# Turning the first batch's token blocks by 16-bit halves and a transposing DMA, in an attention and mixer kernel on one core

## The chip, the cores and the metric

One NeuronCore of one Trainium2 chip. The metric is the device time of one execution in microseconds; 492.01 is the median of three runs before the change (491.93 to 492.79).

## The reference, cut to what matters

```python
x = attn(q, k, v)                       # banded attention, 2 batches, 768 tokens, 512 wide
xt = x.transpose(0, 2, 1)
h = np.maximum(xt @ w_tok1, 0.0) @ w_tok2          # 768 -> 256 -> 768
u = x + h.transpose(0, 2, 1)
h2 = np.maximum(u @ w_ch1, 0.0) @ w_ch2            # 512 -> 1536 -> 512
x = u + h2
...                                     # a third part: rotation by x @ w_theta, a second token mix, w_ch
```

Everything is fp32. The kernel writes each fp32 operand as a high and a low part and makes a product of three matmuls (high x high, high x low, low x high).

## The kernel before, in words

The program has a band branch and a dense branch (`tc.If(band)`, L933); with these inputs the band branch runs. Every engine has its own list of instructions, in the order in which the code is written (`manual_schedule`), and crosses the branch's end by itself.

Inside the branch `attention_band` (L412) walks 24 units of two token blocks each. In unit u PE makes the scores of u, the transposes `t` of u-1 (L485) and the value products `o` of u-2 (L407). Table `fill` puts pieces of the first token mix behind units: `token_part` (L752) adds one block's three matmuls to `mm1`, whose two tiles (`tb` 0 and 1) are emptied by ACT and DVE into `h1`; `token_row` (L772) makes the six matmuls `mm_b_s` of one block of the second product, and DVE adds them to `x` (L787). For batch 0 both lie within the branch. Its turned blocks follow there too: `turn_row` (L789) makes four PE transposes `ut` (L792) of block s, ACT casts them to the high part (L739) and DVE subtracts for the low part (L743). For batch 1 the first product ends the branch and the second, `token_mix2` (L1020), begins the code behind it, with one `tick` after every second block.

Behind it `channel_mix` (L1030) runs 24 steps: `up` makes `gp` from the turned columns (a half of 512 tokens, blocks 0 to 3, then one of 256, blocks 4 and 5), ACT (L707) and DVE (L709) empty it into `g`, and `down` adds 18 matmuls to `h`. `gp` has two PSUM banks, in turn. Batch 1's blocks are turned there by another path: POOL copies a block's 16-bit halves apart (`halves_out`, L799), SP issues a transposing DMA (L803), POOL copies the halves together again (`halves_join`, L809), then the same ACT cast and DVE subtraction, one block in a step.

The weights arrive as 64-bit words. A `tick` moves every job under way by one phase and starts one: ACT scales (L140, L141), DVE joins (L146, L149) and POOL adds (L150), ACT makes the high part (L158), DVE the low part (L161). `need` ticks until a step's weights are there. `Banks` hands the `acc` tiles out over three PSUM tags in turn.

Of the kernel before, what the change touches and what calls it, by code (L numbers as in the profile page):

```python
# [15 lines left out]
F32 = mybir.dt.float32  # L16
# [4 lines left out]
ALU = mybir.AluOpType  # L21
# [26 lines left out]
GRAIN = 64  # L48
SHIFT = 48
# [34 lines left out]
class Build:  # L84
# [327 lines left out]
    def attention_band(self, pairs_pool, first, h1):  # L412
        nc, tc = self.nc, self.tc
# [5 lines left out]
        with tc.tile_pool(name="au", bufs=2) as up, tc.tile_pool(name="aa", bufs=2) as ap:  # L419
# [118 lines left out]
            N = len(units)  # L538
            fill = collections.defaultdict(list)

            def mix1(b, tb, s, tag):
                return functools.partial(self.token_part, tag, h1, b, tb, s)

            def mix2(s):
                return functools.partial(self.token_row, "m", h1, 0, s)

            def columns(s):
                return functools.partial(self.turn_row, "t", 0, s)

            for n in range(2 * NS):  # L550
                tb, s = divmod(n, NS)
                fill[half + 2 + n // 2].append(mix1(0, tb, s, "m"))
            for s in range(NS):
                fill[N - 4 + s].append(mix2(s))
            for s in range(4):
                fill[N - 2 + s].append(columns(s))
            for tb in range(NT):
                for s in range(NS - 2):
                    fill[N + 1].append(mix1(1, tb, s, "s"))
            self.token_jobs()  # L560
            pairs[order[1]] = self.load_qk(pairs_pool, *order[1], bufs=2)
            for u in range(N + 2):
# [36 lines left out]
                    if oi + 2 < len(order):  # L599
                        pairs[order[oi + 2]] = self.load_qk(pairs_pool, *order[oi + 2], bufs=2)  # L600
            for tb in range(NT):
                for s in range(NS - 2, NS):
                    mix1(1, tb, s, "s")()
            for s in range(4, NS):
                columns(s)()

    def attention_dense(self, pairs_pool, first, h1):

# [3 lines left out]
        with tc.tile_pool(name="du", bufs=2) as up, tc.tile_pool(name="dm", bufs=1) as mp:  # L612
# [3 lines left out]
            t = first  # L616
            for b in range(B):
                for hp in range(NHP):
# [5 lines left out]
                    for i in range(NS):  # L624
# [67 lines left out]
                                    po[:, 0], at, t["v"][:, k], j, k == 0, k == NS - 1  # L692
                                )
                        self.finish_rows(up, po, 1, b, hp, i, "d" + n)
            for bb in range(B):
                for tb in range(NT):
                    for s in range(NS):
                        self.token_part("m", h1, bb, tb, s)
            for s in range(NS):
                self.token_row("m", h1, 0, s)  # L700
                self.turn_row("t", 0, s)

# [66 lines left out]
        if s == NS - 1:  # L769
            self.evac_split(h1[b][:, 0, tb], h1[b][:, 1, tb], mm1, relu=True)  # L770

    def token_row(self, tag, h1, b, s):  # L772

        ps = self.ps.tile([P, E], F32, name="mm2_%d_%d" % (b, s), tag=tag)
        cs = slice(s * P, (s + 1) * P)
        self.mm3(
            ps,
            [
                (
                    (r(self.w2h[:, t, cs]), r(self.w2l[:, t, cs])),  # L780
                    (h1[b][:, 0, t], h1[b][:, 1, t]),
                )
                for t in range(NT)
            ],
        )
        x = self.x[b][:, s, :]
        self.nc.vector.tensor_tensor(out=x, in0=ps, in1=x, op=ALU.add)  # L787

    def turn_row(self, tag, b, s):  # L789
        pt = self.ps.tile([P, NE, P], F32, name="ut_%d_%d" % (b, s), tag=tag)  # L790
        for d in range(NE):
            self.nc.tensor.transpose(pt[:, d, :], self.x[b][:, s, d * P : (d + 1) * P], self.ident)  # L792
        self.columns_split(b, s, pt)

    def halves_out(self, src, t, copy):

# [34 lines left out]
    def split_tile(self, n, name, narrow):  # L831

        if n % 3 != 1:
            return self.ws.tile([P, 2, E], F32, name=name, tag="w", bufs=9)
        m = n // 3
        size = 2 * E + (GRAIN if m == 4 else (SHIFT, GRAIN - SHIFT)[m % 2])
        c0 = (0 if m % 2 else SHIFT) if narrow else (GRAIN - SHIFT if m % 2 else 0)
        w = self.ws.tile([P, size], F32, name=name, tag="n%d" % m)
        return w[:, c0 : c0 + 2 * E].rearrange("p (l e) -> p l e", l=2)

    def early_tile(self, name, i, shift):
        if i != 2:
# [39 lines left out]
    def run(self):  # L882
        nc, tc, dram = self.nc, self.tc, self.dram
        with ExitStack() as es:
# [8 lines left out]
            for b in range(B):  # L893
# [4 lines left out]
            self.mm1 = {}  # L898
# [109 lines left out]
    def moe(self, es, a8s, w12p, h1):  # L1008
        tc = self.tc
        ws = es.enter_context(tc.tile_pool(name="ws", bufs=1, side="right"))  # L1010
        self.moe_jobs(ws, w12p)
        self.prefetch()
        self.token_mix2(h1)
        a8s.close()
        gp = es.enter_context(tc.tile_pool(name="g", bufs=2, side="right"))
        xtp = es.enter_context(tc.tile_pool(name="xt", bufs=1, side="right"))
        tp = es.enter_context(tc.tile_pool(name="tb", bufs=1, side="right"))
        self.channel_mix(gp, PhaseB(self, xtp, tp, gp))

    def token_mix2(self, h1):  # L1020
        for s in range(NS):
            self.token_row("acc", h1, 1, s)
            if s % 2:
                self.tick()

    def columns_out(self, pb, s):
        t = self.turning[s] = pb.scratch("ut_%d" % s, ("cut", "xt0", "xt1")[s % 3])
        self.halves_out(self.x[1][:, s, :], t, self.nc.gpsimd.tensor_copy)

    def channel_mix(self, gp, pb):  # L1030
        nc = self.nc
# [19 lines left out]
        def down(b, k, g):  # L1051
            self.need(self.wc_job[k, 1])
            c2 = self.wc[k][1]
            if k == 0:
                ho[b] = [
                    self.ps.tile([P, E], F32, name="h2_%d_%d" % (b, s), tag="acc") for s in range(NS)
                ]
            for s in range(NS):
                cs = slice(s * P, (s + 1) * P)
                self.mm3(  # L1060
                    ho[b][s],
                    [((g[:, 0, cs], g[:, 1, cs]), (r(c2[0]), r(c2[1])))],
                    first=k == 0,
                    last=k == NF - 1,
                )
# [5 lines left out]
        self.turning = {}  # L1071
# [4 lines left out]
        for i, (b, k) in enumerate(steps):  # L1076
            nxt = up(*steps[i + 1]) if i + 1 < len(steps) else None
            if b == 0:
                if 0 <= k - 4 < NS:
                    self.columns_split(1, k - 4, self.turning.pop(k - 4)[:, 1])  # L1080
                if 0 <= k - 3 < NS:
                    self.halves_join(self.turning[k - 3], nc.gpsimd.tensor_copy)
                if 0 <= k - 2 < NS:
                    self.columns_out(pb, k - 2)
            if b == 1:
                for act, n in plan.get(k, ()):
                    act(n)
            down(b, k, g)
            if b == 1 and k < NF - 1 and k not in (5, 6, 7):
                self.tick()  # L1090
            if (b, k) == (0, NF - 2) or b == 1:
                self.gate += 1
            g = nxt
# [285 lines left out]
```

## Time and profile before

| | us |
|---|---|
| median of three runs | 492.01 (491.93 to 492.79) |
| profiled execution | 491.69 |
| its span, first to last instruction | 489.9 |
| PE busy | 482.7 (99%) |
| DVE busy | 320.0 (65%) |
| ACT busy | 262.6 (54%) |
| POOL busy | 179.2 (37%) |

Busy shares are means over stages. On PE, which overlaps its matmuls, a busy share says little about how well it is fed; the waits, the chain that ended last and the timeline of the stretch say more. Times in the rows are microseconds from the span's start; the chain of waits gives PE's steps by their ends, so it stands some 0.2 us behind the timeline.

### The profile page before, as it was taken

To read this page: it belongs to the slowest core of one execution; us is meant where nothing else is said; L and a number is where in the kernel's file an instruction comes from. 1 tells how busy PE (TensorE), PEld (TensorE's weight loads), DVE (VectorE), ACT (ScalarE), POOL (GpSimd) and SP (SyncE) were. 2 spreads that over 40 slices of the span, in tenths; PEclk is the share of its full clock that TensorE was granted. 3 is DMA by queue.
4 is the path that set the end of the run, shared out by engine and by line. 5 is a ranking of instruction groups with operands and counts; after the bars stand their busy time and mean duration, and the time that the engine had idled before them with its cause. 6 is when DMAs were issued, how large, how long until landed. Compare 5 with 4: busy or idle time off the path is not lost.

```text
span 489.9 us, 7655 instructions
## 1 busy us (share of the span) xinstructions
PE 482.7 (99%) x2836; PEld 409.9 (84%) x2836; DVE 320.0 (65%) x679; ACT 262.6 (54%) x482; POOL 179.2 (37%) x187
## 2 busy tenths in 40 slices
PE   8999999999999999999999999999999999999997
PEld 4888888788888888888888888888888889988896
DVE  4688788854776699606756564687998876351442
ACT  6798777723565554204569464646776556322010
POOL 7346433430443565401423241334554643333000
PEclk9999999999999999999999999999999999999999
DMA  6686864301453545302444322433310111000012
GB/s 193 208 266 218 281 207 119 127 2 39 147 169 107 165 133 155 83 1 86 145 134 149 88 51 64 136 95 93 79 23 21 40 26 23 21 23 22 23 72 100
DMA packets 49022, 50.66 MB, mean 103 GB/s; under 512 B 20944, under 2 KB 39888, under 8 KB 48976
## 3 DMA queue, kind: packets, MB, share of 16 engines
q1 hardware_dynamic: 48976, 50.08, 34.4%
q8 instruction: 25, 0.41, 0.4%
q14 instruction: 21, 0.17, 0.1%
HBM read 42.21 MB, written 3.15 MB: 93 GB/s over the span
## 4 chain that ended last, share of the span: by engine, by line
PE 86%; DVE 5%; ACT 5%; POOL 1%; DMA 1%; issue 1%; SPq 0%; DVEq 0%; ACTq 0%
PE gp L97 20%; PE h L97 18%; PE y L97 13%; PE v L97 7%; PE mm L97 7%; PE o L407 6%; PE t L485 5%; PE s L438 5%; PE th L97 5%; DMA q<-q 1%; ACT cut_xt L809 1%; DVE x L1068 1%; DVE w L1159 1%; POOL s L1185 1%; ACT cvt L140 1%
## 5 line engine op out<-in xcount | busy, mean ns | idle before, releaser
L150 POOL TENSOR_TENSOR cvt<-cvt,cvs 128x512 int32<-128x512 int32 (+1 forms) x57 | 75.0, 1317 | 176.9 <-DVE cvt L149 146.9
L97 PE MATMUL h<-wc,g 128*128 128x512 f32 x432 | 102.0, 390 | 0.0
L97 PE MATMUL gp<-xh,wc 128*128 128x512 f32 (+1 forms) x384 | 96.1, 333 | 0.0
L97 PEld LDWEIGHTS h<-wc,g 128*128 128x128 f32 x432 | 79.5, 188 | 15.6
L97 PEld LDWEIGHTS gp<-xh,wc 128*128 128x128 f32 x384 | 66.7, 188 | 8.6 <-DVE g L709 0.2
L709 DVE SCALAR_TENSOR_TENSOR g<-gp,g 128x512 fp32r<-128x512 f32 (+1 forms) x48 | 26.7, 555 | 61.4 <-ACT g L707 61.4
L97 PE MATMUL gp<-xl,wc 128*128 128x512 f32 (+1 forms) x192 | 63.1, 334 | 0.0
L97 PE MATMUL y<-wri,s 128*128 128x512 f32 (+1 forms) x288 | 51.6, 334 | 0.4 <-POOL s L1185 0.4
L707 ACT ACTIVATE g<-gp 128x512 fp32r<-128x512 f32 (+1 forms) x48 | 23.4, 488 | 52.9 <-PE gp L97 52.9
L97 PE MATMUL y<-wri,z 128*128 128x512 f32 (+1 forms) x288 | 51.5, 333 | 0.0
L485 PE MATMUL t<-ident,e 128*128 128x128 f32 x176 | 48.1, 285 | 1.0 <-ACT at L497 1.0
L97 PEld LDWEIGHTS y<-wri,s 128*128 128x128 f32 x288 | 43.5, 188 | 6.4 <-POOL s L1185 0.8
L97 PEld LDWEIGHTS y<-wri,z 128*128 128x128 f32 x288 | 43.7, 188 | 5.8
L146 DVE SCALAR_TENSOR_TENSOR cvs<-cvt,cvs 128x512 int32<-128x512 int32 (+1 forms) x57 | 43.2, 758 | 0.0
L97 PEld LDWEIGHTS gp<-xl,wc 128*128 128x128 f32 x192 | 36.0, 188 | 4.8
L485 PEld LDWEIGHTS t<-ident,e 128*128 128x128 f32 x176 | 31.7, 184 | 8.9 <-ACT at L497 2.7
L451 DVE CUSTOM_DVE_ANT_0 e<-s,base 128x256 f32<-128x256 f32 (+1 forms) x96 | 32.9, 398 | 8.5 <-PE s L438 7.0
L140 ACT ACTIVATE cvt<-raw 128x512 f32<-128x512 f32 (+1 forms) x57 | 37.1, 652 | 2.3 <-issue 2.3
L141 ACT ACTIVATE cvs<-raw 128x512 int32<-128x512 uint16 (+1 forms) x57 | 37.3, 654 | 0.0
L97 PE MATMUL th<-s,xt 128*128 128x512 f32 x144 | 34.9, 391 | 0.1
L1162 ACT ACTIVATE w<-w 128x512 f32<-128x512 f32 x12 | 7.6, 633 | 48.3 <-DVE w L1159 48.3
L407 PE MATMUL o<-v,at 128*128 128x65 f32 x192 | 32.3, 252 | 0.0
(111 smaller groups left out, 843.1 us busy)
## 6 DMA issues: line engine op xcount, KB each, us to landing
raw<-w_ch SPq DMA_DIRECT2D x28, 512.0 KB, 4.1
raw<-w_tok SPq DMA_DIRECT2D x21, 512.0 KB, 4.2
k<-k SPq DMA_DIRECT2D x7, 480.0 KB, 5.6
v<-v SPq DMA_DIRECT2D x8, 384.0 KB, 3.9
out<-o SPq DMA_DIRECT2D x11, 256.0 KB, 2.0
q<-q SPq DMA_DIRECT2D x7, 384.0 KB, 4.9
raw<-w_theta SPq DMA_DIRECT2D x4, 512.0 KB, 4.0
a<-v SPq DMA_DIRECT2D x8, 240.0 KB, 4.7
```

What stands on the lines that cost most here:

```text
L97: self.nc.tensor.matmul(out, lhsT=a, rhs=b, start=first and i == 0, stop=last and i == n - 1)
L140: nc.scalar.activation(out=f(t), in_=f(top), func=AF.Copy, scale=2.0**-111)
L141: nc.scalar.activation(out=s, in_=nxt, func=AF.Copy, scale=2.0**-13)
L146: nc.vector.scalar_tensor_tensor(out=s, in0=t, scalar=-(1 << 31), in1=s, op0=ALU.bitwise_and, op1=ALU.bitwise_or)
L150: nc.gpsimd.tensor_tensor(out=t, in0=t, in1=s, op=ALU.add)
L407: self.nc.tensor.matmul(po[:, j * OW : j * OW + D + 1], lhsT=at, rhs=v[:, j * (D + 1) : (j + 1) * (D + 1)], start=first, stop=last,)
L438: nc.tensor.matmul(ps[j][:, ii, c0:], lhsT=t["q"][pj, i * P : (i + 1) * P], rhs=kf[pj, i * KW - P + c0 : i * KW + P], start=True, stop=True,)
L451: nc.vector.tensor_tensor_reduce(out=e, in0=ps[j][:, ii, c0:], in1=self.base[2 * hp + j][min(i, 1)], op0=ALU.add, op1=ALU.min, scale=-SCAL ...
L485: nc.tensor.transpose(pt[:, ii, c, :], e[j][:, ii, c * P : (c + 1) * P], self.ident)
L707: nc.scalar.activation(out=hi, in_=ps, func=AF.Relu if relu else AF.Copy)
L709: nc.vector.scalar_tensor_tensor(out=lo, in0=ps, scalar=0.0, in1=f(hi), op0=ALU.max, op1=ALU.subtract)
L1162: nc.scalar.activation(out=a, in_=t, func=AF.Abs)
```

## The change

Batch 0's six blocks no longer go over PE. `token_mix2`, behind the branch, opens with POOL's halves of blocks 0 to 3, then their joins, then the same for blocks 4 and 5; the DMA is issued by `halves_out`. Batch 1's second product is taken in two passes over the two halves of its inner length (five rows, then the same five, then row 3 whole), and casts, subtractions and additions stand behind it in a new order. The two `tick`s that are left out there come after the first `down`. In the branch the second tile of batch 1's `mm1` now follows the first as a whole. The blocks' buffers are those that later weight pieces use.

```diff
@@ attention_band @@
             def mix2(s):
-                return functools.partial(self.token_row, "m", h1, 0, s)
-
-            def columns(s):
-                return functools.partial(self.turn_row, "t", 0, s)
+                def step():
+                    self.token_row("m", h1, 0, s)
+                    self.token_add(0, s)
+
+                return step
...
-            for s in range(4):
-                fill[N - 2 + s].append(columns(s))
-            for tb in range(NT):
-                for s in range(NS - 2):
-                    fill[N + 1].append(mix1(1, tb, s, "s"))
+            for s in range(NS - 2):
+                fill[N + 1].append(mix1(1, 0, s, "s"))
...
             for tb in range(NT):
-                for s in range(NS - 2, NS):
+                for s in range(0 if tb else NS - 2, NS):
                     mix1(1, tb, s, "s")()
-            for s in range(4, NS):
-                columns(s)()
@@ token_row, token_add, turn_row @@
-    def token_row(self, tag, h1, b, s):
-
-        ps = self.ps.tile([P, E], F32, name="mm2_%d_%d" % (b, s), tag=tag)
+    def token_row(self, tag, h1, b, s, parts=range(NT)):
+
+        if (b, s) not in self.mm2:
+            self.mm2[b, s] = self.ps.tile([P, E], F32, name="mm2_%d_%d" % (b, s), tag=tag)
...
+    def token_add(self, b, s):
         x = self.x[b][:, s, :]
-        self.nc.vector.tensor_tensor(out=x, in0=ps, in1=x, op=ALU.add)
-
-    def turn_row(self, tag, b, s):
-        pt = self.ps.tile([P, NE, P], F32, name="ut_%d_%d" % (b, s), tag=tag)
-        for d in range(NE):
-            self.nc.tensor.transpose(pt[:, d, :], self.x[b][:, s, d * P : (d + 1) * P], self.ident)
-        self.columns_split(b, s, pt)
+        self.nc.vector.tensor_tensor(out=x, in0=self.mm2.pop((b, s)), in1=x, op=ALU.add)
@@ token_mix2 @@
+        pool = self.nc.gpsimd.tensor_copy
         for s in range(NS):
-            self.token_row("acc", h1, 1, s)
-            if s % 2:
-                self.tick()
+            if s < 3:
+                t = self.ws.tile([P, 2, NE, P], F32, name="cut_u0_%d" % s, tag="w", bufs=9)
+            else:
+                t = self.split_raw(s - 1, "cut_u0_%d" % s)[:, 0 : 2 * E]
+                t = t.rearrange("p (l d x) -> p l d x", l=2, d=NE)
+            self.turning[0, s] = t
+        early, late = range(NS - 2), range(NS - 2, NS)
+        for blocks in early, late:
+            for s in blocks:
+                self.halves_out(self.x[0][:, s, :], self.turning[0, s], pool)
+            for s in blocks:
+                self.halves_join(self.turning[0, s], pool)
+        for s in range(NS):
+            self.mm2[1, s] = self.ps.tile([P, E], F32, name="mm2_1_%d" % s, tag="acc")
+        rows = [0, 1, 2, 4, 5]
+        for t in range(NT):
+            for s in rows:
+                self.token_row("acc", h1, 1, s, [t])
+        self.token_row("acc", h1, 1, 3)
+        for s in early:
+            self.columns_turned(0, s)
+        for s in rows[:3]:
+            self.token_add(1, s)
+        self.tick()
+        for s in late:
+            self.token_add(1, s)
+            self.columns_turned(0, s)
+        self.token_add(1, 3)
+
+    def columns_turned(self, b, s):
+        self.columns_split(b, s, self.turning.pop((b, s))[:, 1])
@@ channel_mix @@
             down(b, k, g)
+            for _ in range(2 if i == 0 else 0):
+                self.tick()
```

The order of the built program shows three places. First PE around the end of the branch (`mm_0_5` is the last row of batch 0's second product, `mm_1_0` and `mm_1_1` inside the branch are the two tiles of batch 1's first). Before:

```order
L97 MATMUL mm_0_4_1677<-h_0_80,w_85 128x512 x6
L792 MATMUL ut_2_1685<-ident,x_65 128x128 x4
L407 MATMUL o_1694<-a_3_1386,at_23_1648 128x65
...
L407 MATMUL o_1694<-v_3_1384,at_23_1659 128x65
L97 MATMUL mm_0_5_1709<-h_0_80,w_85 128x512 x6
L792 MATMUL ut_3_1717<-ident,x_65 128x128 x4
L97 MATMUL mm_1_0_1725<-xh_72,w_85 128x512
...
L792 MATMUL ut_4_1767<-ident,x_65 128x128 x4
L792 MATMUL ut_5_1774<-ident,x_65 128x128 x4
L933 UNCONDITIONAL_BRANCH
```

and now:

```order
L97 MATMUL mm_0_4_1661<-h_0_80,w_85 128x512 x5
L407 MATMUL o_1670<-a_3_1386,at_23_1632 128x65 [waits DVE_49,PE_49,Activation_49]
...
L97 MATMUL mm_0_5_1685<-h_0_80,w_85 128x512 x5
L97 MATMUL mm_1_0_1693<-xh_72,w_85 128x512 [waits Pool_49]
...
L97 MATMUL mm_1_1_1714<-xh_72,w_85 128x512
L930 UNCONDITIONAL_BRANCH
```

The transposes are gone from PE's list, and the branch ends with `mm_1_1`.

Second, POOL behind the branch, with the semaphores that each row waits for (`DMAHW` are those of DMAs; `x_65` is batch 0's `x`, `x_66` batch 1's). Before, its first work there is a weight job:

```order
L383 TENSOR_TENSOR xl_73<-x_66,xh_72 128x128 [waits Pool_49]
L933 UNCONDITIONAL_BRANCH
L150 TENSOR_TENSOR cvt_7525<-cvt_7525,cvs_7526 128x512 [waits DVE_49,Activation_49]
L150 TENSOR_TENSOR cvt_7550<-cvt_7550,cvs_7551 128x512 [waits DVE_49,Activation_49]
```

and now:

```order
L930 UNCONDITIONAL_BRANCH
L793 COPY cut_u_0_7417<-x_65 128x1024 [waits DMAHW3_49,DMAHW4_49,DMAHW2_49,DMAHW5_49,DMAHW1_49,DMAHW6_49,DMAHW0_49,DMAHW7_49,PE_49,Activation_49]
L793 COPY cut_u_1_7418<-x_65 128x1024
L793 COPY cut_u_2_7419<-x_65 128x1024
L793 COPY cut_u_3_7420<-x_65 128x1024
L803 COPY cut_u_0_7417<-cut_u_0_7417 128x2x512 [waits DMAHW2_49,Pool_49]
...
L793 COPY cut_u_4_7421<-x_65 128x1024
L793 COPY cut_u_5_7422<-x_65 128x1024 [waits DVE_49]
L803 COPY cut_u_4_7421<-cut_u_4_7421 128x2x512 [waits DMAHW6_49,Pool_49]
L803 COPY cut_u_5_7422<-cut_u_5_7422 128x2x512 [waits DMAHW7_49,Pool_49]
L150 TENSOR_TENSOR cvt_7498<-cvt_7498,cvs_7499 128x512 [waits DVE_49]
```

Twelve copies stand ahead of the first weight job, and the first of them waits for PE, ACT and DMAs.

Third, DVE behind the branch, where eight subtractions of blocks 0 to 3 (L738) come first and then, now:

```order
L787 TENSOR_TENSOR x_66<-mm_1_0_7441,x_66 128x512 [waits PE_49]
L787 TENSOR_TENSOR x_66<-mm_1_1_7442,x_66 128x512 [waits PE_49]
L787 TENSOR_TENSOR x_66<-mm_1_2_7443,x_66 128x512 [waits PE_49]
L787 TENSOR_TENSOR x_66<-mm_1_4_7445,x_66 128x512 [waits DVE_49,PE_49]
L738 TENSOR_TENSOR xl_71<-cut_u_4_7421,xh_70 128x4x128 [waits Activation_49]
L787 TENSOR_TENSOR x_66<-mm_1_5_7446,x_66 128x512 [waits DVE_49,PE_49]
L738 TENSOR_TENSOR xl_71<-cut_u_5_7422,xh_70 128x4x128 [waits Activation_49]
L787 TENSOR_TENSOR x_66<-mm_1_3_7444,x_66 128x512 [waits PE_49]
L704 SCALAR_TENSOR_TENSOR g_0_7521<-gp_0_0_7522,g_0_7521 128x512 [waits Activation_49]
L146 SCALAR_TENSOR_TENSOR cvs_7499<-cvt_7498,cvs_7499 128x512
```

Before, the six additions came first with the joins of two weight jobs among them; now the subtractions of blocks 4 and 5 stand behind four and five additions, and the first join behind the first `g`.

## Rows read from the trace of the kernel before

**Rows 1.** The page: PE's busy time, and the granted clock in 40 slices.
```profile
PE 482.7 (99%) x2836; PEld 409.9 (84%) x2836; DVE 320.0 (65%) x679; ACT 262.6 (54%) x482; POOL 179.2 (37%) x187
...
PEclk9999999999999999999999999999999999999999
```

**Rows 2.** Waits of PE, whole span: us in total, times, longest.
```profile
PE t L485 <- ACT at L497: 1.0, 2, 0.6
```

**Rows 3.** The chain that ended last, 84 to 145 us: start, us, what.
```profile
91.85 0.44 PE ut L792 x4
...
94.92 0.12 PE t L485
95.04 0.17 PE o L407 x2
...
95.44 0.25 PE mm L97
...
101.07 1.44 PE mm L97 x6
...
106.12 0.44 PE ut L792 x4
...
114.77 0.87 PE ut L792 x8
```

**Rows 4.** Timeline of PE: start, us, what, count, idle before and releaser.
```profile
106.32 0.48 PE L97 MATMUL mm<-xh,w 128*128 128x512 f32 x1
...
115.81 8.46 PE L97 MATMUL mm<-h,w 128*128 128x512 f32 x36 [0.16 <-issue]
124.10 0.61 PE L97 MATMUL gp<-xh,wc 128*128 128x512 f32 x2
```

**Rows 5.** Timelines of ACT, DVE and POOL around the branch's end.
```profile
118.68 0.66 ACT L140 ACTIVATE cvt<-raw 128x512 f32<-128x512 f32 x1 [2.31 <-issue]
...
115.43 0.69 DVE L709 SCALAR_TENSOR_TENSOR h<-mm,h 128x512 fp32r<-128x512 f32 x1 [0.67 <-ACT h L707]
...
119.52 1.89 DVE L787 TENSOR_TENSOR x<-mm,x 128x512 f32<-128x512 f32 x3 [2.20 <-PE mm L97]
...
123.48 1.30 POOL L150 TENSOR_TENSOR cvt<-cvt,cvs 128x512 int32<-128x512 int32 x1 [16.46 <-DVE cvt L149]
```

**Rows 6.** Tile cut_ut, batch 1's path: duration ns min/median/max, first and last start.
```profile
L743 DVE TENSOR_TENSOR xl<-cut_ut,xh x10: 550/1058/1395, 171.2 to 207.5; 128x384 fp32r<-128x384 f32 x4, 128x128 fp32r<-128x128 f32 x4, 128x512 fp32r<-128x512 f32 x2
L799 POOL COPY cut_ut<-x x6: 1036/1074/1473, 155.3 to 199.3; 128x1024 uint16<-128x1024 uint16 x6
L803 SPq DMA_TRANSPOSE cut_ut<-cut_ut x6: 1237/1241/1727, 156.3 to 200.8; - x6
L809 POOL COPY cut_ut<-cut_ut x6: 1343/1564/1718, 163.4 to 203.7; 128x1024 uint16<-128x1024 uint16 x6
L739 ACT CAST xh<-cut_ut x6: 603/610/622, 170.5 to 206.9; 128x512 fp32r<-128x512 f32 x6
...
DMA to landing us min/median/max: 2.7/2.7/3.1
```

**Rows 7.** Timelines of DVE and POOL, 170 to 178 us.
```profile
171.20 2.37 DVE L743 TENSOR_TENSOR xl<-cut_ut,xh 128x384 fp32r<-128x384 f32 x2 [0.80 <-ACT xh L739]
...
171.77 1.72 POOL L809 COPY cut_ut<-cut_ut 128x1024 uint16<-128x1024 uint16 x1
```

**Rows 8.** POOL's timeline, and busy tenths of the DMA engines from 200.5 by 0.1 us.
```profile
203.70 1.34 POOL L809 COPY cut_ut<-cut_ut 128x1024 uint16<-128x1024 uint16 x1 [2.90 <-DMA cut_ut<-cut_ut]
...
DMA  0000000000000003999999999200901088930019
```

**Rows 9.** Weight jobs and `g`: the page, tile wc, and groups from 118 to 142 us.
```profile
L709 DVE SCALAR_TENSOR_TENSOR g<-gp,g 128x512 fp32r<-128x512 f32 (+1 forms) x48 | 26.7, 555 | 61.4 <-ACT g L707 61.4
...
L161 DVE SCALAR_TENSOR_TENSOR wc<-cvt,wc x5: 681/682/1677, 128.3 to 140.9; 128x512 fp32r<-128x512 f32 x5
...
L146 DVE SCALAR_TENSOR_TENSOR cvs<-cvt,cvs 128x512 int32<-128x512 int32 x7 | 4.8, 682 | 0.0
...
L149 DVE TENSOR_SCALAR cvt<-cvt 128x512 int32<-128x512 int32 x6 | 2.6, 428 | 0.2
```

More of the change, by code (lines that the diff above doesn't have):

```diff
@@ L694, in attention_dense @@
                         self.finish_rows(up, po, 1, b, hp, i, "d" + n)
-            for bb in range(B):
                 for tb in range(NT):
                     for s in range(NS):
[L698 to L701, printed above, removed]
+                        self.token_part("m", h1, b, tb, s)
+                for s in range(NS if b == 0 else 0):
+                    self.token_row("m", h1, 0, s)
+                    self.token_add(0, s)
     def evac_split(self, hi, lo, ps, relu=False):
@@ L770, in token_part @@
             self.evac_split(h1[b][:, 0, tb], h1[b][:, 1, tb], mm1, relu=True)
-    def token_row(self, tag, h1, b, s):
-        ps = self.ps.tile([P, E], F32, name="mm2_%d_%d" % (b, s), tag=tag)
+    def token_row(self, tag, h1, b, s, parts=range(NT)):
+        if (b, s) not in self.mm2:
+            self.mm2[b, s] = self.ps.tile([P, E], F32, name="mm2_%d_%d" % (b, s), tag=tag)
         cs = slice(s * P, (s + 1) * P)
         self.mm3(
-            ps,
+            self.mm2[b, s],
             [
@@ L782, in token_row @@
                 )
-                for t in range(NT)
+                for t in parts
             ],
+            first=0 in parts,
+            last=NT - 1 in parts,
         )
+    def token_add(self, b, s):
         x = self.x[b][:, s, :]
-        self.nc.vector.tensor_tensor(out=x, in0=ps, in1=x, op=ALU.add)
-    def turn_row(self, tag, b, s):
-        pt = self.ps.tile([P, NE, P], F32, name="ut_%d_%d" % (b, s), tag=tag)
-        for d in range(NE):
-            self.nc.tensor.transpose(pt[:, d, :], self.x[b][:, s, d * P : (d + 1) * P], self.ident)
-        self.columns_split(b, s, pt)
+        self.nc.vector.tensor_tensor(out=x, in0=self.mm2.pop((b, s)), in1=x, op=ALU.add)
     def halves_out(self, src, t, copy):
@@ L835, in split_tile, with split_raw @@
         m = n // 3
+        c0 = (0 if m % 2 else SHIFT) if narrow else (GRAIN - SHIFT if m % 2 else 0)
+        w = self.split_raw(m, name)
+        return w[:, c0 : c0 + 2 * E].rearrange("p (l e) -> p l e", l=2)
+    def split_raw(self, m, name):
         size = 2 * E + (GRAIN if m == 4 else (SHIFT, GRAIN - SHIFT)[m % 2])
-        c0 = (0 if m % 2 else SHIFT) if narrow else (GRAIN - SHIFT if m % 2 else 0)
-        w = self.ws.tile([P, size], F32, name=name, tag="n%d" % m)
-        return w[:, c0 : c0 + 2 * E].rearrange("p (l e) -> p l e", l=2)
+        return self.ws.tile([P, size], F32, name=name, tag="n%d" % m)
     def early_tile(self, name, i, shift):
@@ L897, in run @@
                 self.ut.append((self.columns_of(2 * b, hi), self.columns_of(2 * b + 1, lo)))
-            self.mm1 = {}
+            self.mm1, self.mm2 = {}, {}
             self.ps = Banks(es.enter_context(tc.tile_pool(name="ps", bufs=1, space=PSUM)))
@@ L1012, in moe @@
         self.prefetch()
+        self.turning = {}
         self.token_mix2(h1)
@@ L1020, in token_mix2 @@
     def token_mix2(self, h1):
+        pool = self.nc.gpsimd.tensor_copy
         for s in range(NS):
-            self.token_row("acc", h1, 1, s)
-            if s % 2:
-                self.tick()
+            if s < 3:
[26 more added lines that the diff above has]
+        self.token_add(1, 3)
     def columns_out(self, pb, s):
-        t = self.turning[s] = pb.scratch("ut_%d" % s, ("cut", "xt0", "xt1")[s % 3])
+        t = self.turning[1, s] = pb.scratch("ut_%d" % s, ("cut", "xt0", "xt1")[s % 3])
         self.halves_out(self.x[1][:, s, :], t, self.nc.gpsimd.tensor_copy)
+    def columns_turned(self, b, s):
+        self.columns_split(b, s, self.turning.pop((b, s))[:, 1])
     def channel_mix(self, gp, pb):
@@ L1070, in channel_mix @@
         g = up(*steps[0])
-        self.turning = {}
         plan = {2: [(pb.turn_out, 0)], 3: [(pb.turn_in, 0), (pb.turn_low, 0), (pb.turn_out, 1)],
@@ L1079, in channel_mix @@
                 if 0 <= k - 4 < NS:
-                    self.columns_split(1, k - 4, self.turning.pop(k - 4)[:, 1])
+                    self.columns_turned(1, k - 4)
                 if 0 <= k - 3 < NS:
-                    self.halves_join(self.turning[k - 3], nc.gpsimd.tensor_copy)
+                    self.halves_join(self.turning[1, k - 3], nc.gpsimd.tensor_copy)
                 if 0 <= k - 2 < NS:
```

## The prediction

> **What bounds the kernel now.** The page comes first: TensorE (PE) is busy 99% of the span at full clock [rows 1], so time can only come off PE's own queue or be lost in new holes in it. The list of what PE waited for is next: after the start its largest entry is two waits for ACT's copies, 1.0 us together [rows 2]. Everything below therefore asks two things: how much PE work goes, and when the data of the next PE instruction is ready. The chain of waits runs on PE through the whole stretch that the change touches, except around 96 to 99 us, where it steps over to ACT; there the reader sees the transposes `ut` that are removed, with what each adds to the chain [rows 3]. PE's timeline gives the landmarks: first matmul of batch 1's first token mix at 106.32, the 36 matmuls of its second from 115.81, the first `gp` matmul, which needs batch 0's turned columns, at 124.10 [rows 4].
>
> **What goes.** Twenty-four transposes leave PE. Blocks 0, 2 and 3 cost 0.44 us each in the chain, blocks 4 and 5 together 0.87 [rows 3]. Block 1 lies beside waits: from 95.44 to 101.07 the chain has 5.63 us, of which 1.45 are six `mm` matmuls and about 2.3 the 8 transposes and 16 value products of unit 23 (8 x 0.12 and 8 pairs x 0.17 by the unit ahead of it). That leaves 1.9 us of `ut` and of waiting for the copy `at`. The wait should go with it: DVE's bias step of unit 23 started only after block 0's two subtractions, and PE's scores came 0.44 us behind the transposes; both are gone, which brings ACT's chain about 1 us forward, while PE needs that copy only some 0.6 us later than it would then be done. So PE starts batch 1's mix 3 x 0.44 + 1.9 = 3.2 us sooner, at 103.1, and stands before `gp` 3.2 + 0.87 = 4.1 us sooner, at **120.0**. If the two waits stayed whole (1.0 us), it would be 3.1. Moving the rest of `mm1` (the second token block now goes after the first) and taking `mm2` by halves moves no PE work: 36 and 36 matmuls before and after, and the row whose PSUM bank is still being emptied goes last.
>
> The Trainium skill (TensorE: Matmul & The Clock Gate, Part 4: PE-mode transpose) has a transpose at about 275 ns inside a kernel. By it 24 would be 6.6 us; the rows show 0.11 us each in the chain, 2.6 in all, because they overlap, so the trace decides and the sum does not use the page.
>
> **What comes, and when it is ready.** POOL gets twelve copies, SP six transposing DMAs; ACT's casts and DVE's subtractions move behind them. Their durations are in the rows of the same path for batch 1 [rows 6]: copy out 1.04, transposing DMA 1.24 on SP, copy back 1.34, cast 0.61. Step by step, in the trace's clock:
>
> 1. POOL's first copy writes into memory that the branch used, and its wait names PE. The wait's count is one number for both arms of the branch, whose counts are made to end alike; counting PE's updates in the built program, in this arm it falls on the 15th matmul of batch 1's first `mm1` tile. PE's 36 take 8.29 us, 0.23 each [rows 4], so that is 103.1 + 3.5 + 0.2 of drain = 106.8. POOL itself would be through the branch by then: an engine that crosses it stands 2.2 to 2.3 us [rows 5], and its last band work, which ended at 107.0 before (123.48 less 16.46 of idling), ends at about 104.
> 2. Four copies out, each started 0.94 after the last: done at 107.9, 108.8, 109.8, 110.7. SP issues a DMA every 1.3 us; a copy back starts 2.90 us after the issue [rows 8]. One DMA keeps the engines busy for some 1.0 us [rows 8], less than the issue pitch, so I let four follow each other unhindered. Copies back: 110.8, 112.1, 113.4, 114.7, the last done at 116.1.
> 3. DVE is through its band work and the branch at 111.4 (end of `mm1`) + 0.6 + 0.7 + 2.2 = 115.0 [rows 5], ACT a little sooner. Now both ends meet: a DVE subtraction with both inputs in SBUF doesn't run while POOL runs a copy. At 171.20 two of them took 2.37 and ended with POOL's copy, which itself took 1.72; the shortest of the path are 0.55 and 1.34 [rows 6, 7]. So the pairs of the four early blocks alternate with POOL: the first piece at 116.1, block 4's copy out 116.4 to 117.5, second piece, block 5's 117.6 to 118.6, then the rest while POOL waits for the DMA, the last at about 120.4. PE needs it for its third `gp` matmul, 120.0 + 0.46. No stall, but nothing to spare.
> 4. Blocks 4 and 5: DMAs from 117.5 and 118.8, copies back at 120.4 and 121.8, the second done at 123.1 to 123.2. DVE's order has three additions at 0.61 [rows 5] first, then block 4's, then its subtraction, block 5's addition and subtraction: 120.6 + 4 x 0.61 = 123.0; the subtraction waits for POOL until 123.2, done 123.75; the addition 124.35; block 5's subtraction (cast done 123.8) **125.0**.
> 5. PE has finished the 512-wide half of `gp` at 120.0 + 12 x 0.23 = 122.8. The 256-wide half needs block 5's cast for its first matmul and its subtraction for the second: 125.0. PE stands 125.0 - 122.8 - 0.1 = **2.1 to 2.2 us**.
>
> Sum: 4.1 - 2.2 = 1.9 us sooner from there on.
>
> **What is late next.** The two conversion steps that moved from the second mix to after the first `down` start the weight pieces of step 2 later: their first POOL addition stood at 123.48 [rows 5] and now follows POOL's last copy back and DVE's `g` at about 127. I walked the chain (DVE 0.68 and 0.43, POOL 1.30, an ACT cast, then DVE 0.68 to 1.68 when POOL holds it [rows 5, 9]) with the two extra steps: the first piece is whole at 132, needed at 134.5; the piece for step 3 at 137, needed at 142.7; `g` of step 2 leaves PSUM at 142.5, when PE wants that bank at 142.7. So it just holds, and DVE idled 61.4 us ahead of `g` over the 24 steps [rows 9], 2.6 a step, so the lag runs out. Cost taken: nothing; bound: 1 to 2 us.
>
> Against the profiled execution of 491.69 us this makes 489.8. The median of the runs, 492.01, lies 0.3 above it, so I say **490.1**. Anything within 0.2% (1 us) would not be told from no change.
>
> **Rivals.**
> - *The columns are earlier than I walk.* If POOL and DVE get by each other (subtractions at 0.55, the lower end of the row's range [rows 6]), block 5 is ready near 123.9 and the stall is about 1.1; without any stall the gain is 4.1. Times 489.0 down to 487.9. For it: some subtractions of the row did run at 550 ns. Against: most did not.
> - *The conversions run late.* Step 2's `g` or step 3's weights hold PE another 1 to 2 us, and the gain is given back: 491 to 492. For it: 0.2 us of slack in my walk at 142.5. Against: DVE's idle time in each later step [rows 9].
> - *Transposing DMAs don't follow each other.* All six in the trace stand alone [rows 6]; no row shows two in flight. If each waits for the one ahead to land (2.75 us), block 3's copy back starts at 119, block 5's at 126.8 and PE's second half at 129.6: a stall of 6.8, 2.7 us **slower** than before, 494.7. It decides from where a pitch of more than about 1.8 us makes the stall over 4.1. Against: the engines' busy 1.0 us per DMA.
> - *The copies don't start ahead of the branch's end.* If the wait on PE fell on the branch's last matmul, 21 matmuls or 4.8 us later, everything above shifts: also slower, by about 3, 495. The count speaks against it; I add it to the last one.
>
> **How the numbers follow.** The walk as it stands, with a gain of 1.0 to 2.9: 0.50. Earlier columns, gain over 2.9: 0.16. Late conversions, within 1 us of before: 0.20. DMAs in line or a late start, slower: 0.14. Faster by over 0.2% is then 0.66, within it 0.20, slower 0.14. For eight in ten I take the walk, most of the earlier columns (down to a gain of 3.6, 488.4) and most of the late conversions (up to 492.3), and leave out the slow cases.
>
> **What the new profile would show.** Right: `gp` starts near 120, PE idles about 2 us ahead of the first 256-wide `gp` matmuls, put down to DVE's subtraction or ACT's cast; POOL's first copy near 106.8; SP issues at 1.3 us. Wrong: an idle PE at the first 512-wide `gp`, or copies back more than 1.4 us apart with POOL waiting for the DMA (DMAs in line); PE waiting for DVE between 134 and 144 (conversions); no wait at all at the 256-wide half (earlier columns).

## The result and the profile after

The changed kernel takes 496.19 us (median, 495.10 to 497.21) against 492.52 for the kernel before on the same chip: a ratio of 1.0083, 95% interval 1.0072 to 1.0094, so about 4 us **slower**. Forecast was 490.1 (488.4 to 492.3), faster. The profiled span is 494.2 us, 4.3 above that of before.

The page of the changed kernel, busy time and granted clock (the speed that TensorE was allowed, in tenths of full speed), against [rows 1]:

```profile
PE 483.4 (98%) x2812; PEld 408.7 (83%) x2812; DVE 324.9 (66%) x679; ACT 263.2 (53%) x482; POOL 195.1 (39%) x199
...
PEclk9999999999899999999999999999999999999999
```

PE has 24 instructions fewer and is busy for longer; one slice shows an 8 where before all were 9. The list of PE's waits says where, against [rows 2]:

```profile
PE gp L97 <- DVE xl L738: 2.8, 2, 2.2
PE gp L97 <- ACT xh L734: 1.4, 1, 1.4
...
PE mm L97 <- DVE h L704: 0.7, 1, 0.7
...
PE o L407 <- DVE x L400: 0.5, 1, 0.5
```

The waits for ACT's `at` are gone as forecast, and 4.2 us of new waiting stand inside the first `gp` product. The timelines of PE, POOL, ACT and DVE put them in order (start, us, what, count, idle before and releaser), against [rows 4, 5]:

```profile
113.83 7.79 PE L97 MATMUL mm<-h,w 128*128 128x512 f32 x33 [0.74 <-DVE h L704]
121.45 0.61 PE L97 MATMUL gp<-xh,wc 128*128 128x512 f32 x2
124.24 0.50 PE L97 MATMUL gp<-xl,wc 128*128 128x512 f32 x1 [2.17 <-DVE xl L738]
...
128.23 0.39 PE L97 MATMUL gp<-xh,wc 128*128 128x256 f32 x1 [1.41 <-ACT xh L734]
129.28 0.38 PE L97 MATMUL gp<-xl,wc 128*128 128x256 f32 x1 [0.66 <-DVE xl L738]
...
112.21 1.33 POOL L803 COPY cut_u<-cut_u 128x1024 uint16<-128x1024 uint16 x1 [0.44 <-DMA cut_u<-cut_u]
116.34 4.27 POOL L803 COPY cut_u<-cut_u 128x1024 uint16<-128x1024 uint16 x3 [2.81 <-DMA cut_u<-cut_u]
120.53 2.38 POOL L793 COPY cut_u<-x 128x1024 uint16<-128x1024 uint16 x2
124.92 2.61 POOL L803 COPY cut_u<-cut_u 128x1024 uint16<-128x1024 uint16 x2 [2.01 <-DMA cut_u<-cut_u]
...
116.76 0.62 ACT L734 CAST xh<-cut_u 128x512 fp32r<-128x512 f32 x1 [3.72 <-DMA cut_u<-cut_u]
...
118.54 5.85 DVE L738 TENSOR_TENSOR xl<-cut_u,xh 128x384 fp32r<-128x384 f32 x8 [4.76 <-DMA cut_u<-cut_u]
124.31 2.47 DVE L787 TENSOR_TENSOR x<-mm,x 128x512 f32<-128x512 f32 x4
```

PE stands twice: 2.17 us at the third 512-wide matmul, which needs the low parts of blocks 0 to 3, and 1.41 + 0.66 at the 256-wide half. Behind it POOL's second copy back comes 4.1 us after the first, not 1.3, after 2.81 of waiting for a DMA. ACT's first cast comes 3.2 us after its block is joined (112.21 + 1.33), and DVE's first subtraction at 118.5, with the releaser given as a DMA that had long landed: both were still on their way out of the branch. These crossings took 3.7 and 4.8 us where before they took 2.3 and 2.2.

The table of stretches (us, PE, PEld, DVE, ACT, POOL busy, granted clock, DMA share, GB/s) shows the 8 of the page:

```profile
127.00:129.00 2.00, 0.39 (x1) 0.19 (x1) 2.00 (x3) 1.44 (x3) 0.53 (x1) 1.00 1.07 393
129.00:131.00 2.00, 1.72 (x9) 1.72 (x10) 2.00 (x4) 0.79 (x2) 0.00 (x0) 0.67 0.11 27
131.00:133.00 2.00, 2.00 (x8) 1.71 (x7) 1.32 (x4) 0.51 (x2) 1.28 (x1) 0.50 0.80 251
133.00:135.00 2.00, 2.00 (x9) 1.59 (x9) 0.82 (x2) 1.62 (x3) 1.07 (x1) 0.98 0.01 5
```

After the stalls PE got half its clock (1.2 instead of 2.4 GHz) from about 129.7 until about 133. All five executions of the changed kernel show it in their mean clock, 0.993 to 0.997, where all but two of more than 70 recorded executions of the kernel before have 0.999 or 1.0. An estimate fits this: 3.4 us at half speed in a span of 494.2 give a mean of 0.997. Step 0's first `h` matmul starts at 136.4 where it was 132.6, and the last `h` matmul of the kernel at 330.9 against 327.0: the loss is made here and kept. Last, the six DMAs (tile `cut_u`), and what moved on the DMA queues from 108 to 118 us, against [rows 6]:

```profile
L797 SPq DMA_TRANSPOSE cut_u<-cut_u x6: 1232/1312/2266, 108.8 to 122.9; - x6
...
DMA to landing us min/median/max: 2.9/3.6/5.4
```

```profile
q1 hardware_dynamic: 4224, 1.05, 89.4%
q14 instruction: 4, 0.03, 1.6%
q8 instruction: 2, 0.03, 1.4%
```

They land 2.9 to 5.4 us after the issue instead of 2.7 to 3.1. Six packets of instruction code (the two queues of kind `instruction`, q8 and q14) share the DMA engines with the first four.

### The profile page after: what moved, and what is told of

Same layout as the page of the kernel before. It is cut to its first block, busy times and chain, and to the rows that moved or that the text cites. A ratio compares the mean times of both kernels' runs of the same rounds, so it can differ in the third digit from the quotient of the medians.

```text
span 494.2 us, 7639 instructions
## 1 busy us (share of the span) xinstructions
PE 483.4 (98%) x2812; PEld 408.7 (83%) x2812; DVE 324.9 (66%) x679; ACT 263.2 (53%) x482; POOL 195.1 (39%) x199
## 4 chain that ended last, share of the span: by engine, by line
PE 83%; DVE 6%; ACT 4%; POOL 3%; DMA 2%; issue 1%; DVEq 0%; POOLq 0%; ACTq 0%
PE gp L97 20%; PE h L97 18%; PE y L97 13%; PE v L97 7%; PE o L407 6%; PE s L438 5%; PE th L97 5%; PE t L485 4%; PE mm L97 4%; DMA cut_u<-cut_u 2%; PE warm L331 1%; POOL cut_u L803 1%; POOL cut_u L793 1%; ACT cut_xt L803 1%; DVE x L1095 1%
## 5 line engine op out<-in xcount | busy, mean ns | idle before, releaser
L97 PE MATMUL gp<-xh,wc 128*128 128x512 f32 (+1 forms) x384 | 97.5, 337 | 1.4 <-ACT xh L734 1.4
L97 PEld LDWEIGHTS gp<-xh,wc 128*128 128x128 f32 x384 | 67.7, 191 | 10.6 <-ACT xh L734 1.8
L146 DVE SCALAR_TENSOR_TENSOR cvs<-cvt,cvs 128x512 int32<-128x512 int32 (+1 forms) x57 | 45.3, 794 | 0.3 <-ACT cvs L141 0.2
```

Of the source, the lines that this page charges most:

```text
L97: self.nc.tensor.matmul(out, lhsT=a, rhs=b, start=first and i == 0, stop=last and i == n - 1)
L146: nc.vector.scalar_tensor_tensor(out=s, in0=t, scalar=-(1 << 31), in1=s, op0=ALU.bitwise_and, op1=ALU.bitwise_or)
```

## The experiments

Theory after this look, against the single rival "transposing DMAs don't follow each other": the DMAs and the code that ACT, DVE and PE fetch as they leave the branch delay each other; the stalls that follow cost PE its clock; and the parts of the change that only reorder work may cost something of their own. Medians stand beside 492.0 to 492.2 for the kernel before in the same sessions, with the ratio's 95% interval.

**Filling PE's stalls.**

```diff
+                if (b, k) == (0, 0):
+                    for _ in range((9, 18)[h]):
+                        nc.tensor.matmul(
+                            ps, lhsT=r(self.w1h[:, 0, 0:P]),
+                            rhs=r(self.xh[1][:, 0, 0 : hs.stop - hs.start]), start=True, stop=True,
+                        )
                 self.mm3(ps, terms, low_last=h == 0)
```

> The changed kernel with extra matmuls in PE's two stalls of the first gp: 9 of 128x512 (9 x 0.23 = 2.1 us) ahead of its 512-wide half and 18 of 128x256 (2.1 us) ahead of its 256-wide half, into the PSUM tile that the real matmuls then overwrite. They make no data earlier. Theory (the clock is the second part of the loss): in the changed kernel the granted clock leaves full speed after PE's two stalls, from 129.7 to 133.1, and that costs about 1.7 us; with the stalls filled it stays at full speed, h of step 0 starts near 134.8 instead of 136.5, and the time is 494.2 to 494.7. Rival (the clock costs nothing here because the lateness of the data decides, or it falls for another reason): 496.0 to 496.5, or a clock that falls as before.

495.42 us, 1.0074 (1.0062 to 1.0086). The stretches and PE's waits:

```profile
129.00:131.00 2.00, 1.85 (x15) 1.63 (x14) 2.00 (x4) 0.96 (x3) 0.00 (x0) 1.00 0.07 26
131.00:133.00 2.00, 2.00 (x11) 1.64 (x10) 1.97 (x4) 0.36 (x2) 1.28 (x1) 1.00 0.78 259
```

```profile
PE gp L97 <- DVE g L704: 0.8, 1, 0.8
```

The time lies between the two cases. The clock stays whole and `h` starts at 134.8, 1.6 sooner: the price of the clock, as expected. The mean clock is 1.0 in all six executions, where the changed kernel had none above 0.997, so the filling is what kept the clock. Only half of it reached the end, because a wait for `g` of 0.84 us at 148.1 appeared that the slow clock had covered. The gain at the end, 0.8 us in the medians and 0.4 by the ratios, isn't clear of noise, since the two ratios' intervals overlap.

**All copies out first.**

```diff
-        for blocks in early, late:
-            for s in blocks:
-                self.halves_out(self.x[0][:, s, :], self.turning[0, s], pool)
-            for s in blocks:
-                self.halves_join(self.turning[0, s], pool)
+        for s in range(NS):
+            self.halves_out(self.x[0][:, s, :], self.turning[0, s], pool)
+        for s in range(NS):
+            self.halves_join(self.turning[0, s], pool)
```

> The changed kernel with all six copies out and their DMAs ahead of the six copies back (POOL's list alone changes). Theory A (blocks 4 and 5 are late because POOL issues them only behind four joins, which wait for slow DMAs): block 5 is joined near 122 instead of 126.3, PE no longer stands ahead of the 256-wide half (2.1 us less), the stall at the 512-wide half stays near 2, and the clock may then hold (1.7 more): 492.3 to 494.2. Theory B (transposing DMAs in flight together delay each other, about 2.7 us each): six in line from 110 land at 126, block 5 joined at 127.5 or later, 497 or more.

495.38 us, 1.0071 (1.0059 to 1.0083): a miss for both. Block 5 was joined at 123.7, 3.8 us sooner than now, so B falls; but PE still stood 2.71 and 1.69 us for DVE, whose eight subtractions took 6.4 us from 118.8 and whose additions followed:

```profile
125.00 0.50 PE L97 MATMUL gp<-xl,wc 128*128 128x512 f32 x1 [2.71 <-DVE xl L738]
129.40 0.39 PE L97 MATMUL gp<-xl,wc 128*128 128x256 f32 x1 [1.69 <-DVE xl L738]
```

POOL's list was not what held the second half; DVE was. In this trace the clock stayed at full speed, with 4.4 us of stalls against the changed kernel's 4.2. But three of the run's six executions have a mean clock of 0.992 to 0.997: the same kernel goes either way, and what decides it is left open.

**Transposes back on PE, the rest of the change kept** (`turn_row` and its places as before; `halves_out`, `halves_join` and `columns_turned` out of `token_mix2`).

> The transposes go back onto PE, at their places in the branch as before the change; all else of the change stays (the second mm1 tile behind the first, mm2 in two passes with row 3 last, additions in the new order, two ticks behind the first down). Theory (the whole loss is the late columns): 491.7 to 492.7, no different from before by more than 0.7. Rival (the reordering and the moved ticks cost something themselves, for instance the wait of 0.7 us for row 1's PSUM bank): 493 or more.

494.03 us, 1.0041 (1.0028 to 1.0054): the rival holds. The reordering alone, with no DMA path, makes the kernel 2.0 us slower. PE's timeline:

```profile
116.86 0.49 PE L97 MATMUL mm<-h,w 128*128 128x512 f32 x1 [0.29 <-ACT xh L742]
117.70 8.23 PE L97 MATMUL mm<-h,w 128*128 128x512 f32 x35 [0.35 <-DVE xl L746]
...
130.21 0.73 PE L97 MATMUL gp<-xh,wc 128*128 128x512 f32 x2 [0.18 <-DVE g L712]
147.85 0.74 PE L97 MATMUL gp<-xh,wc 128*128 128x512 f32 x2 [0.96 <-DVE g L712]
```

Four waits, 1.78 us, that the kernel before doesn't have (it has 0.16 at the first of these places [rows 4]): two ahead of the second product, two for `g`. This doesn't simply add to the cost of the late columns: in the changed kernel PE comes to `gp` too early anyway, so the wait ahead of the second product only shortens the stall there, and `g` is covered.

**The two ticks elsewhere** (the kernel above, with one edit).

```diff
-            for _ in range(2 if i == 0 else 0):
+            if i in (8, 9):
                 self.tick()
```

> The kernel of run e3_pe_all (transposes back on PE, the rest of the change kept) with the two conversion steps taken from behind the first down to behind the downs of steps 8 and 9. Theory (the two ticks there crowd DVE ahead of g, which PE then waits for, 1.1 us; the other part of e3's 2.0 us is the second mm1 tile, 0.6): 492.6 to 493.2. Rival (the g waits come from the conversions being late as a whole, not from these two ticks in that place): 493.8 or more, with the waits for g still there or grown, or weights late.

493.42 us, 1.0025 (1.0015 to 1.0036). The wait of 0.96 is gone, that of 0.18 stays; the time fell by 0.6 rather than 1.1, between the two. The ticks behind the first `down` cost that wait; how much of it reached the time is less sure, since the two ratios' intervals overlap. The rest is mostly the other waits.

**The DMAs later.** Eight more POOL copies (fp32, into a tile that is overwritten) ahead of the first copy out.

```diff
+        for _ in range(8):
+            pool(out=self.turning[0, 0][:, 1].rearrange("p d x -> p (d x)"), in_=self.x[0][:, 0, :])
         for blocks in early, late:
```

> The changed kernel with eight more POOL copies (8 x 0.95 = 7.6 us, into a tile that the real copy then overwrites) ahead of the first copy out, so that the four DMAs follow each other at 116 to 121, after all engines are through the branch. Meant for the DMAs' data phases alone. Theory A (the DMAs at 109 to 118 were slowed by something else that ran then, such as the engines' code fetches at the branch's end): data phases of 1.1 to 1.4 us each, copies back 1.3 to 1.5 apart, first copy back about 2.9 after its issue; time some 5 to 6 above the changed kernel, 501 to 502. Theory B (DMAs in flight together slow each other): data phases of 1.9 to 2.7 as before, copies back as far apart as now (4.1, 1.4, 1.3), time 503 to 504.

498.64 us (one run), lower than either theory said: the extra copies took 0.61 us each and followed each other every 0.67, not 0.95, and DVE's first subtraction came only 1.8 us later than now. The time itself says little here, since PE's clock was half for some 6 us of this trace as well; the run is there for its DMAs. The DMAs, from 114.3 to 121 us:

```profile
q1 hardware_dynamic: 4224, 1.05, 80.3%
q14 instruction: 2, 0.02, 0.9%
```

```profile
L797 SPq DMA_TRANSPOSE cut_u<-cut_u x6: 1232/1307/1337, 114.4 to 126.3; - x6
...
DMA to landing us min/median/max: 2.8/3.1/3.8
```

With two code packets in the way instead of six, four transposing DMAs follow each other at the issue pitch: landings 2.8 to 3.8, and POOL's copies back without a gap (four in 5.43 us). So they do follow each other, and theory B falls. In the other direction, without transposing DMAs (run e3_pe_all, transposes back on PE) ACT crossed in 1.98 us, against 3.72 in the changed kernel:

```profile
119.28 0.66 ACT L140 ACTIVATE cvt<-raw 128x512 f32<-128x512 f32 x1 [1.98 <-issue]
```

That the code packets are what is in the way is inferred from the queue counts; no run took the packets themselves away. The count alone doesn't decide it either: in the next run six code packets fall between 108 and 118 us, as many as in the changed kernel, and the DMAs land in 2.8 to 4.0 us.

**The second `mm1` tile behind the branch.**

```diff
@@ attention_band @@
-            for tb in range(NT):
-                for s in range(0 if tb else NS - 2, NS):
-                    mix1(1, tb, s, "s")()
+            for s in range(NS - 2, NS):
+                mix1(1, 0, s, "s")()
@@ attention_dense @@
-                for tb in range(NT):
+                for tb in range(NT - b):
@@ token_mix2, ahead of mm2 @@
+        for s in range(NS):
+            self.token_part("s", h1, 1, 1, s)
```

> The changed kernel with one edit: the second mm1 tile of batch 1 (18 matmuls and its emptying by ACT and DVE) stands behind the branch instead of at its end, in both arms. ACT and DVE then have their last work in the branch 4.1 us sooner (at about 109 and 109.7) and cross while PE works on that tile. Theory (ACT's first cast at 116.8 and DVE's first subtraction at 118.5 are late because their crossings, 3.7 and 4.8 us beside the transposing DMAs, come last): the first subtraction starts by 116 and the third gp matmul 1 to 2 us sooner than 124.2; the second half still waits for blocks 4 and 5. 494.5 to 495.7. Rival (the DMAs' landing alone holds the columns): first subtraction at 118 or later, 496 or more.

494.52 us, 1.0060 (1.0046 to 1.0075), as expected, at the lower edge. The timelines of PE, ACT and DVE:

```profile
122.61 0.51 PE L97 MATMUL gp<-xl,wc 128*128 128x512 f32 x1 [0.97 <-DVE xl L737]
127.20 0.38 PE L97 MATMUL gp<-xh,wc 128*128 128x256 f32 x1 [2.00 <-ACT xh L733]
...
114.36 0.62 ACT L733 CAST xh<-cut_u 128x512 fp32r<-128x512 f32 x1 [0.70 <-POOL cut_u L802]
...
115.01 1.85 DVE L737 TENSOR_TENSOR xl<-cut_u,xh 128x384 fp32r<-128x384 f32 x2 [0.63 <-ACT xh L733]
```

ACT and DVE cross while PE works; the first subtraction starts at 115.0 instead of 118.5, PE's first stall shrinks from 2.17 to 0.97, and the DMAs land in 2.8 to 4.0. The second stall grows from 2.07 to 2.66 (2.00 and 0.66), because PE now gets there 1.6 sooner and the columns only 1.0. The clock stays whole in this trace, but five of the run's six executions have a mean clock of 0.997 like the changed kernel, so the gain on the changed kernel (1.7 us in the medians, 1.1 by the ratios, whose intervals just overlap) isn't the clock's.

**Fewer blocks by DMA.** The last eight runs share a base: the two ticks behind downs 8 and 9, all copies out first, subtractions ahead of most additions, and blocks that aren't listed turned by PE as before.

| run | blocks by DMA | besides | us | interval of the ratio |
|---|---|---|---|---|
| v1 | 1 to 5 | row 1 last | 493.46 | 1.0017 to 1.0040 |
| v2 | 2 to 5 | row 1 last | 492.12 | 0.9992 to 1.0010 |
| v3 | 3 to 5 | row 1 last | 490.90 | 0.9973 to 0.9991 |
| v5 | 3 to 5 | rows 0, 4, 5, 1, 2, 3 | 490.49 | 0.9952 to 0.9984 |
| v7 | 2 to 5 | same rows, tile behind the branch | **490.27** | 0.9954 to 0.9980 |
| v8 | 1 to 5 | same as v7 | 491.75 | 0.9981 to 1.0005 |
| v10 | 1 to 5 | v8, four additions behind `g` | 490.83 | 0.9965 to 0.9985 |
| v11 | 0 to 5 | same as v10 | 492.29 | 0.9994 to 1.0013 |

```diff
-        for s in range(NS):
+        turned = [2, 3, 4, 5]
+        for s in turned:
...
-        rows = [0, 1, 2, 4, 5]
+        rows = [0, 4, 5, 1, 2]
...
+        self.columns_turned(0, 2)
+        self.columns_turned(0, 3)
+        self.token_add(1, 0)
+        self.columns_turned(0, 4)
+        self.token_add(1, 4)
+        self.columns_turned(0, 5)
...
@@ up, v10 and v11 @@
+                for s in (5, 1, 2, 3) if (b, k, h) == (0, 0, 0) else ():
+                    self.token_add(1, s)
```

The edits are those of v7 and, in the last two lines, of v10 and v11. Expected of v1, v2 and v3:

> Only blocks 1 to 5 of batch 0 go by POOL and DMA, block 0 stays on PE; all copies out ahead of the copies back; row 1 (whose PSUM bank is the last to be emptied) last instead of row 3; the two ticks behind downs 8 and 9; subtractions ahead of most additions on DVE. PE saves 3.65 us (5 blocks and most of the waits for at); by the theory the columns of block 5 are turned near 125.5 where PE wants them near 123, a stall of 2 to 2.5 us in all: 490.5 to 491.5. If the DMAs and code fetches still stand in each other's way as in the changed kernel and DVE shares with POOL: 492 to 493.

> As v1_12345 with blocks 0 and 1 on PE and blocks 2 to 5 by POOL and DMA. PE saves 1.75 us (blocks 2, 3: 0.44 each, 4 and 5: 0.87); the last block is joined about 1.4 us sooner and wanted 1.9 later than there: no stall over 0.7. 490.3 to 491.2. If the stalls stay: 492 or more.

> As v1_12345 with blocks 0 to 2 on PE and blocks 3 to 5 by POOL and DMA. PE saves 1.3 us and nothing stalls: 490.7 to 491.2. If the rest of the change (second mm1 tile behind the first, ticks) still costs: 491.5 to 492.5.

v3 came as expected. v2 came at its upper case and v1 0.5 above it, each block more about 1.3 us dearer: DVE, late out of the branch at 119.7 to 120.4 in all three, reached `g` behind all subtractions and additions, and PE waited 1.4 for it in v1 and v2 and not in v3. Block 1 also gave PE less than the 1.9 us counted for it: with it gone, the 1.0 us of waits for `at` comes back as a wait for DVE to empty an `o` tile (v1, and v8 and v10 below):

```profile
PE o L407 <- DVE x L400: 1.0, 1, 1.0
```

In v3 one new wait was left ahead of the second product, whatever the rows' order:

```profile
115.80 7.79 PE L97 MATMUL mm<-h,w 128*128 128x512 f32 x33 [0.74 <-DVE h L711]
```

The pool hands its banks out in the order of first use, so the second row always got the bank of the second `mm1` tile, and row 3 last (or row 1) changed nothing.

> Run v3_345 with the rows of the second product taken as 0, 4, 5, 1, 2 and 3 last: there the second row got the PSUM bank of the second mm1 tile in whatever order the rows came, and PE stood 0.73 us; now that bank comes fourth, after 9 matmuls. Theory: the wait of 0.7 goes and nothing takes its place, v3's time less 0.7: 490.0 to 490.4. Rival (columns or g become the wait): 490.7 to 491.2.

> Run v2_2345 with the rows of v5_345_rows and the second mm1 tile behind the branch as in e6_cross. If the crossings of ACT and DVE are what made the columns and then g late there (1.4 us of waiting for g), both waits go: v2's time less 0.7 and less 1.4: 489.5 to 490.5. If not: 491 to 492.

> As v7_2345_cross with block 1 by DMA too. By the theory v1's 493.5 less 0.7 (row's bank) and less most of its 0.7 and 1.4 at gp: 490.5 to 491.5; if the DMAs alone hold the columns: 492.5 or more.

v5 has no such wait; its 490.49 is 0.1 above the range. v7 and v8 came in theirs or 0.25 above. In v7 PE has no wait over 0.15 us from 101 us to the end of step 0, and it is 1.7 us **faster** than before (1.0 to 2.3 by the ratio's interval), which agrees with the whole of what its four blocks cost on PE (0.44 + 0.44 + 0.87). v5 and v7 can't be told apart by time; that the fourth block pays is read from the traces alone, where `h` starts at 131.28 in v7 and 131.52 in v5. v8, with five blocks, left a wait for `g` (1.5); the last two runs moved additions behind `g`:

> Run v8_12345_cross with the last four additions behind g's first half. There PE waited 1.47 us for g, which stood on DVE behind four additions (2.47 us). If that was all that held v8 back, 491.75 less 1.4: 490.1 to 490.7. If the additions then hold the PSUM banks of the first down, or the columns become the wait: 491 to 492.

> All six blocks by POOL and DMA as in the changed kernel, with every cost found so far taken out: second mm1 tile behind the branch, all copies out first, rows 0, 4, 5, 1, 2, 3, the two ticks behind downs 8 and 9, and the last four additions behind g's first half instead of ahead of it. If the four causes (crossings beside DMAs, clock, ticks, the row's bank) are all there was: PE's 3.65 less a stall of about 2 for the columns of six blocks, 490 to 491. If six blocks are too many for POOL and DVE in that time: a stall of 3 us or more at gp, 491.5 to 493.

v10 was 0.9 better than v8 and 0.1 above its range; it can't be told from v7, so a fifth block added nothing that shows. v11 came at its second case by its time, with a stall of 1.9 for the columns (and 0.8 for `g`), not the 3 expected there. PE, DVE and POOL in v11:

```profile
123.67 0.50 PE L97 MATMUL gp<-xl,wc 128*128 128x512 f32 x1 [1.90 <-DVE xl L744]
...
115.67 8.15 DVE L744 TENSOR_TENSOR xl<-cut_u,xh 128x384 fp32r<-128x384 f32 x8 [1.15 <-ACT xh L740]
...
115.53 7.06 POOL L815 COPY cut_u<-cut_u 128x1024 uint16<-128x1024 uint16 x5 [0.54 <-DMA cut_u<-cut_u]
```

DVE is out of the branch in time there and works without a gap, but beside POOL's five copies the eight pieces take 8.15 us. A pair took 0.76 in v7 where POOL was idle, so four would take some 3.0:

```profile
116.38 0.76 DVE L744 TENSOR_TENSOR xl<-cut_u,xh 128x384 fp32r<-128x384 f32 x2 [0.27 <-ACT xh L740]
```

Six blocks were too many for this stretch in each of the orders tried.

## Why the prediction was wrong

- **What goes** held in kind: no `ut`, no waits for `at`. PE reached batch 1's mix at 104.07, not 103.1: it now ran ahead of DVE's emptying of an `o` tile (0.47), and this trace stood 0.24 behind already ahead of the first `ut` that is gone (its `mm` matmuls start at 90.45, before at 90.21). "Moving the rest of `mm1` ... moves no PE work" was true and not enough: the second tile now ends right ahead of the second product, and "the row whose PSUM bank is still being emptied goes last" was wrong, since the bank goes by order of use: 0.74. So `gp` began at 121.45, not 120.0.
- **Step 1**, POOL's wait on the 15th matmul, held: its first copy started at 107.8, 1.0 after the forecast, as PE was.
- **Step 2 failed first**: "I let four follow each other unhindered". Copies back came at 112.2, 116.3, 117.7 and 119.1 instead of 110.8 to 114.7. In place of a steady 2.9 us from the issue to the copy back, the first four DMAs landed up to 5.4 us after it; that fetched code is the reason is inferred. The rivals of DMAs in line (494.7) and of a late start (495) had the nearest times, but by luck: apart from the branch's end four DMAs do follow each other, and POOL's copies did start ahead of it.
- **Step 3 failed with it**: DVE was through the branch at 118.5, not 115.0, and the last early piece was done at 124.3, not 120.4. "No stall, but nothing to spare" became 2.17 us. Of the 3.5 us, 1.0 is PE's own lateness. The rest is the crossing: the 2.2 to 2.3 of [rows 5] was taken as fixed, and beside the DMAs it took 3.7 and 4.8.
- **Steps 4 and 5** had the size right (2.07 at the 256-wide half, against 2.1 to 2.2), but 4.3 later. That is luck: the columns came 4.2 later than forecast, and PE, held up by the steps before, about as much (126.8 instead of 122.8).
- **Not in the sum at all**: the clock, 1.6. The sum at `h` is then 1.4 at the start of `gp`, 2.2 for the first stall, 0.1 less for the second, 1.6 for the clock, and 0.6 because the matmul behind each of the three waits starts 0.15 to 0.3 later than the wait alone explains. This is 5.7 us against a forecast gain of 1.9: 3.8 slower at `h`, as seen.
- **What is late next**, costed at nothing, was worth 0.6 to 1 us (the move of the ticks), in its bound; the changed kernel doesn't show it, because PE comes later there. The traces of e1, e2 and e6, whose clock stays whole, have a wait for `g` of 0.84 in its place.

The Trainium skill (Runtime: NRT & Kernel Launch, Instruction fetch mechanics) says that a taken branch whose target isn't near has its code fetched by DMA before the engine goes on. The 2.0 to 2.3 us for which an engine stands in an undisturbed crossing agree with such a stop. That it takes 3.7 and 4.8 beside other DMAs is what this case adds. The Trainium skill (SBUF — State Buffer, SBUF: two separate sides) has DVE with two SBUF inputs and GpSimd hold a port pair in turn, each blocking the other; the 8.15 us against 3.0 agree.

## What to carry to other kernels

Before work is put behind a branch's end, price the crossing of every engine that has to feed it, and don't start a train of small-packet DMAs in the same microseconds: give the engines that feed it their last work in the branch earlier, so that they cross under PE's work. Work taken off a full PE pays only as far as the engines that take it over deliver on time: four of six blocks paid what they had cost on PE, a fifth added nothing that shows, and the sixth gave it back. And run an edit that only reorders by itself: here it cost 2 us alone, 1.8 of it in waits behind a tile that ended too late and two weight steps that crowded DVE.

## What the runs showed of the hardware that was not expected

- Transposing DMAs from SP follow each other at the issue pitch of 1.3 us and land in 2.8 to 3.8 us away from the branch's end (run e4_late), but in up to 5.4 (5.8 in e2_all_out) beside it; ACT and DVE, which cross there, lose 1.4 and 2.6 us. That the fetched code is the reason is inferred.
- Stalls of PE of 4.2 us in three pieces within 8 us were followed by 1.2 GHz for some 3.4 us in the changed kernel, in all five executions by their mean clock. Stalls of 4.4 us in two pieces were followed by none in the trace of e2_all_out, but three of that kernel's six executions have a mean clock of 0.992 to 0.997: near such stalls one kernel can go either way.
